# Expert operands asked for earlier in the order of a block, and one constant tile put at the head of its pool

## The chip, the cores and the metric

One core of a Trainium2 chip runs the kernel. The metric is the device time of one execution in microseconds. The engines are TensorE (PE in the profile, with its weight loads as PEld), VectorE (DVE), ScalarE (ACT), GpSimd (POOL) and SyncE (SP), which here only issues DMAs. Each engine works through its own queue in order and waits for the others by semaphores.

## What is computed

Three layers follow each other: linear attention with an exponential feature map, a soft mixture of experts with four slots for each of eight experts, and a dense mixture of eight experts whose weights P come from a gate that is normalised over rows and columns eight times. Only the last one matters here:

```python
def _moe2_ref(x, w_gate, w1, w2):        # x: 2304 x 512, 8 experts, hidden width 1024
    logits = x @ w_gate
    P = np.exp(logits - logits.max())
    for _ in range(8):
        P /= P.sum(1, keepdims=True) + 1e-09
        P /= P.sum(0, keepdims=True) + 1e-09
        P *= N / E
    out = np.zeros((N, D), dtype=np.float32)
    for e in range(E):
        h = np.maximum(x @ w1[e], 0.0)
        ye = h @ w2[e]
        out += P[:, e:e + 1] * ye
    return out
```

## The kernel before

**First layer.** The second layer's output has only 32 distinct rows behind it (its slots), so x is never formed: x @ w1[e] is the 2304 x 32 matrix of combine weights times a small product of slot outputs and w1[e]. The combine weights lie transposed in five tiles, ct0 to ct3 with 512 tokens each and ct4 with the last 256 (line 520 on). Each value is split into a high and a low part, stacked over the 128 rows. For an expert, `make_stack` computes the small product (matmuls ps, 32 of them), splits it, and `spread_stack` brings it into the form `st` that the first layer takes as its stationary operand (matmuls pr, two copies st<-pr on ACT). `first_layer(i, n)` is four matmuls of 256 tokens against ct; a block has two of these, together eight matmuls z<-ct,st.

**Blocks and products.** Tokens go in nine blocks of 256 for each expert, 72 blocks i in all, block after block and expert after expert (e, blk). The second layer, h @ w2[e], is one step of a scheme that needs seven products of half-size matrices instead of eight. Products 0 to 6 use the left operands a11, a12, s2, s1, s3, s4, a22 (made from the block's hidden values by `hidden`) and the right operands b11, b21, t2, t1, t3, b22, t4 (made from w2[e]). In the profile a right operand is w_b where it is a block of w2 itself (operands 0, 1, 5) and w_t where it is a sum (2, 3, 4, 6). Products 0, 2, 4 and 6 go into the sum x, 1 into z, 3 and 5 into y. Each product is 12 matmuls of 128 x 128 against 256 columns: four parts of the hidden width, each with high times high, high times low and low times high. After each product DVE adds its share, scaled by P, to the output tile xo (`take`). The sums lie in four PSUM buffers that are taken in turn.

**Hidden values.** `hidden(i + 1)` runs during block i. It is a generator of five steps, one after each of the products 2 to 6, and its first step comes after the first layer of block i + 1, which stands behind product 2 of block i. It makes r22, s1, s2, r11, s4, s3 as raw tiles (tag s, three buffers, so that s4 takes over the buffer of s1 and s3 that of s2), the high parts hh on ACT, and the low parts hl: those of a11, a12, a22 on DVE, those of s1, s2, s4, s3 on POOL (hl_s).

**Right operands.** The loop is written out by hand: from line 505 on, every instruction stays in program order on its engine, and all of them carry line 50 in the profile, that of the helper that records them. Two tables say behind which product of which block the next expert's operands are asked for:

```python
    W_SUMS = {(3, 1): 0, (3, 6): 1, (5, 6): 2, (7, 6): 3}
    W_PARTS = {(2, 6): 0, (4, 6): 2, (6, 6): 1, (8, 1): 3, (8, 6): 4, (9, 0): 5, (9, 1): 6}
```

A key is (block, product); blocks from 9 on mean blocks of the expert itself, so (9, 1) is behind product 1 of its own block 0. `w_sum(e, n)` is one subtraction or addition of 128 x 1024 on POOL: sum 0 makes t1 in the place of b11, sum 1 t2, sum 2 t3 in the place of b12, sum 3 t4 in the place of b21. `w_part(e, k)` makes operand k: a cast on ACT (its high part) and a subtraction on POOL (its low part). The operands lie in ten buffers, and operand k of expert e takes buffer (7e + k) mod 10. So operand 3 takes the buffer of the running expert's operand 0, 4 that of 1, 5 that of 2 and 6 that of 3; the last reader of each is that product in block 8.

**Order within a turn of the loop.** After product k and its take come, in this order: the next expert's stack (block 8, behind product 0) and its spreading (behind product 1), the next first layer (behind product 2), a step of `hidden`, a sum, a part, and two scalings of output rows on ACT in expert 0's block 8 and in expert 1.

**Weights.** SP loads the two units of w2 and the two of w1 of the next expert at the end of block 0 (1 MB each), into buffers that are freed when the last operand of the running expert has been made.

**The pool const.** It is the first pool on its side and lives for the whole kernel. Its tiles lie behind each other in the order in which their tags are first used: ident, ones (512 bytes per partition each), wg (128), si (2048), x0 to x5 (2048 each; later ct0 to ct3 and rep0, rep1 in the same places), rd_held (line 279; 16 bytes, which take 32), ct4 (1024). It begins at byte 16512 of a partition, and ct4 at 32032.

Of the kernel before, what the change touches and what calls it, by code (L numbers as in the profile page):

```python
# [8 lines left out]
F32R = mybir.dt.float32r  # L9
# [44 lines left out]
def tile_kernel(ctx: ExitStack, tc: tile.TileContext, a):  # L54
# [3 lines left out]
    const = ctx.enter_context(tc.tile_pool(name="const", bufs=1, side="left"))  # L58
# [8 lines left out]
    def load_const(name, shape, pool=None, q=SP):  # L67
        t = (pool or const).tile(shape, F32, name=name, bufs=1)
        q.dma_start(out=t, in_=a[name])
        return t  # L70
# [32 lines left out]
    def load_k(t):  # L103
        x = kp.tile([128, 512], F32, tag="kt", name=f"kt{t}")
        SP.dma_start(out=x, in_=a["kT"][t])
        kt_t[t] = x

    def load_v(i):
        x = kp.tile([128, 512], F32, tag="vt", name=f"vt{i}", bufs=3)
        SP.dma_start(out=x, in_=a["vb"][i])  # L110
        vt_t[i] = x
# [287 lines left out]
    load_k(1)  # L399
    load_v(0)  # L400
    load_k(2)
    ident = load_const("ident", [128, 128])
    ones = load_const("ones", [128, 128])
    sel_e = load_const("sel_e", [128, 4], kp)
# [113 lines left out]
    mp = mp_cm.__enter__()  # L518

    ct = [const.tile([128, 512], F32R, tag=f"x{i}", name=f"ct{i}", bufs=1) for i in range(4)]  # L520
    ct.append(const.tile([128, 256], F32R, name="ct4", bufs=1))
    rep = [const.tile([128, 4, 128], F32R, tag=f"x{4 + i}", name=f"rep{i}", bufs=1) for i in range(2)]
    for i in range(2):
        G.dma_start(out=rep[i], in_=a["rep"][:, i * 512:(i + 1) * 512].rearrange("p (g c) -> p g c", g=4))
# [99 lines left out]
    def w_sum(e, n):  # L624


        w = wsrc[e]
        if n == 0:
            G.tensor_tensor(out=w["t1"], in0=w["t3"], in1=w["b11"], op=ALU.subtract)
        elif n == 1:  # L630
            G.tensor_tensor(out=w["t2"], in0=w["t1"], in1=w["b22"], op=ALU.subtract)
        elif n == 2:
            G.tensor_tensor(out=w["t3"], in0=w["t3"], in1=w["b22"], op=ALU.subtract)
        else:
            G.tensor_tensor(out=w["t4"], in0=w["t4"], in1=w["t2"], op=ALU.add)

    def w_part(e, k):

        name = PRODUCTS[k][1]
        s = wsrc[e][name]  # L640
        n = (7 * e + k) % NW
        w = (cl1 if n < 4 else cl2).tile([128, 2, KH, 256], F32R, tag=f"wo{n}", name=f"w{e}_{name}", bufs=1)
        A.copy(out=w[:, 0], in_=s)
        G.tensor_tensor(out=w[:, 1], in0=s, in1=w[:, 0].bitcast(F32), op=ALU.subtract)
        wop[e, k] = w
        if k == 6:
            wsrc.pop(e)
            for n in range(2):
                unit_t.pop(("moe2_w2", e, n))
# [284 lines left out]
        pass  # L934
    load_munits(4)

    W_SUMS = {(3, 1): 0, (3, 6): 1, (5, 6): 2, (7, 6): 3}
    W_PARTS = {(2, 6): 0, (4, 6): 2, (6, 6): 1, (8, 1): 3, (8, 6): 4, (9, 0): 5, (9, 1): 6}
    SINK = {1: 3, 5: 2}
    making = iter(())  # L940
    for i, (e, blk) in enumerate(blocks):
# [3 lines left out]
        for k in range(7):  # L945
# [10 lines left out]
            next(making, None)  # L956
            if more and (blk, k) in W_SUMS:
                w_sum(e + 1, W_SUMS[blk, k])
            if more and (blk, k) in W_PARTS:
                w_part(e + 1, W_PARTS[blk, k])  # L960
            if e and (blk + 9, k) in W_PARTS:
                w_part(e, W_PARTS[blk + 9, k])
            if e == 0:
# [72 lines left out]
```

## Time and profile before

| | us |
|---|---|
| median of 3 runs | 1088.23 |
| lowest and highest | 1085.76, 1088.39 |
| the profiled execution, its own time | 1086.3 |
| its span, first to last instruction | 1084.1 |
| mean granted TensorE clock (share of full speed) | 0.995 |

| engine | busy, share of the span | instructions |
|---|---|---|
| PE | 1052.2 us, 97% | 9206 |
| DVE | 732.0 us, 68% | 1518 |
| POOL | 687.3 us, 63% | 442 |
| ACT | 569.8 us, 53% | 1009 |

The attention takes the first 230 us, the second layer's experts the stretch up to some 270 us, and the loop over 72 blocks the rest. Matmuls are pipelined: a record of 0.28 us follows the one before it after 0.11 us, so that the start of one to the start of the next is the measure of PE's pace, and a merged line of the timeline ("x8") gives the start of its first. In the timeline the brackets hold the engine's idle time before the line and what ended it. In the chain, a piece is a run of instructions of one kind, each following on the one before.

### The profile page before, as it was taken

How to read it: one execution, taken by the hardware profiler on the slowest of the kernel's cores; microseconds unless marked ns; L12 is line 12 of the kernel's file. 1: busy time of each engine (PE TensorE's matmuls, PEld its weight loads, DVE VectorE, ACT ScalarE, POOL GpSimd, SP SyncE). 2: the span in 40 equal slices, each digit the busy share in tenths (PEclk: the TensorE clock that was granted, in tenths of full speed). 3: DMA queues.
4: the chain of work that ended last, by engine and by line, in shares of the span. 5: the costliest groups of instructions: out<-in, count | busy, mean ns of one | idle time of the engine just before them, and what ended most of it. 6: DMA issues, size and time to landing. Idle time of an engine off the chain costs nothing.

```text
span 1084.1 us, 23152 instructions
## 1 busy us (share of the span) xinstructions
PE 1052.2 (97%) x9206; PEld 982.0 (91%) x9206; DVE 732.0 (68%) x1518; ACT 569.8 (53%) x1009; POOL 687.3 (63%) x442
## 2 busy tenths in 40 slices
PE   7999999999899999999999999999999999999998
PEld 5688788853899999999999999999999999999998
DVE  6878777850578767665766666576667666665765
ACT  5665544312556576654556454655555564545542
POOL 4776551107556777777777577767777775777443
PEclk9999999999899999999999999999999999999999
DMA  7772115379400130022003100300220031000111
GB/s 264 246 272 88 54 40 205 146 279 399 158 2 2 36 121 1 2 79 79 2 1 117 40 2 16 141 2 1 79 79 1 2 112 46 2 1 21 54 45 60
DMA packets 22571, 89.26 MB, mean 82 GB/s; under 512 B 2752, under 2 KB 5568, under 8 KB 14272
## 3 DMA queue, kind: packets, MB, share of 16 engines
q1 hardware_dynamic: 22176, 87.26, 22.2%
q8 instruction: 73, 1.20, 0.5%
q0 software_dynamic: 288, 0.52, 0.2%
q14 instruction: 34, 0.28, 0.1%
HBM read 83.05 MB, written 4.72 MB: 81 GB/s over the span
## 4 chain that ended last, share of the span: by engine, by line
PE 78%; POOL 11%; DVE 5%; issue 2%; DMA 2%; ACT 1%; SPq 0%; POOLq 0%; DVEq 0%; ACTq 0%
PE x L50 30%; PE y L50 14%; PE z L50 12%; PE num L271 6%; POOL hl_s L50 5%; POOL w_t L50 3%; PE kvacc L179 3%; POOL w_b L50 2%; PE ut L246 1%; PE ps L50 1%; DVE s L50 1%; PE kvp L218 1%; DMA moe_w<-in_moe_w 1%; PE pk L142 1%; PE ph L50 1%
## 5 line engine op out<-in xcount | busy, mean ns | idle before, releaser
L50 POOL TENSOR_TENSOR hl_s<-s,hh_s 128x512 fp32r<-128x512 f32 x288 | 367.5, 1298 | 230.1 <-ACT hh_s L50 214.0
L50 PE MATMUL x<-w_t,hh_s 128*128 128x256 f32 x1152 | 205.4, 278 | 3.9 <-DVE xo L50 2.7
L50 ACT ACTIVATE hh_s<-s 128x512 fp32r<-128x512 f32 x288 | 175.7, 629 | 53.0 <-DVE s L50 49.1
L50 PEld LDWEIGHTS x<-w_t,hh_s 128*128 128x128 f32 x1152 | 173.8, 188 | 5.3 <-issue 3.9
L50 DVE SCALAR_TENSOR_TENSOR xo<-x,P,xo 128x256 f32<-128x256 f32 x252 | 121.1, 481 | 75.3 <-PE x L50 75.3
L50 ACT ACTIVATE hh_a<-z 128x512 fp32r<-128x512 f32 x216 | 122.2, 600 | 90.1 <-DVE s L50 88.3
L50 ACT ACTIVATE r<-z 128x512 f32<-128x512 f32 x144 | 86.1, 598 | 156.6 <-PE z L50 156.2
L50 PE MATMUL x<-w_t,hl_s 128*128 128x256 f32 x576 | 159.7, 277 | 0.0
L50 DVE SCALAR_TENSOR_TENSOR s<-z,r 128x512 f32<-128x512 f32 x144 | 98.9, 687 | 86.7 <-ACT hh_a L50 82.2
L50 DVE SCALAR_TENSOR_TENSOR hl_a<-z,hh_a 128x512 fp32r<-128x512 f32 x216 | 147.4, 683 | 0.0
L50 DVE SCALAR_TENSOR_TENSOR s<-z,s 128x512 f32<-128x512 f32 x144 | 98.5, 684 | 19.4 <-POOL hl_s L50 17.9
L50 PE MATMUL x<-w_t,hh_a 128*128 128x256 f32 x576 | 104.2, 279 | 6.3 <-POOL w_t L50 4.9
L50 PEld LDWEIGHTS x<-w_t,hl_s 128*128 128x128 f32 x576 | 108.3, 188 | 0.0
L50 PE MATMUL y<-w_b,hh_s 128*128 128x256 f32 x576 | 103.8, 278 | 0.2 <-POOL w_b L50 0.2
L50 PE MATMUL x<-w_b,hh_a 128*128 128x256 f32 x576 | 103.1, 279 | 0.0
L50 PE MATMUL z<-w_b,hh_a 128*128 128x256 f32 x576 | 103.0, 279 | 0.0
L50 PE MATMUL y<-w_t,hh_s 128*128 128x256 f32 x576 | 102.9, 278 | 0.0
L50 PEld LDWEIGHTS x<-w_t,hh_a 128*128 128x128 f32 x576 | 87.5, 188 | 7.9 <-POOL w_t L50 6.2
L50 PEld LDWEIGHTS z<-w_b,hh_a 128*128 128x128 f32 x576 | 87.3, 189 | 2.9 <-issue 2.9
L50 PEld LDWEIGHTS y<-w_b,hh_s 128*128 128x128 f32 x576 | 87.5, 188 | 1.4 <-POOL w_b L50 1.3
L50 PEld LDWEIGHTS x<-w_b,hh_a 128*128 128x128 f32 x576 | 87.7, 190 | 0.0
L50 PEld LDWEIGHTS y<-w_t,hh_s 128*128 128x128 f32 x576 | 87.6, 188 | 0.0
(213 smaller groups left out, 2342.1 us busy)
## 6 DMA issues: line engine op xcount, KB each, us to landing
moe_w<-in_moe_w SPq DMA_DIRECT2D x64, 1024.0 KB, 6.9
vt<-in_vb SPq DMA_DIRECT2D x20, 256.0 KB, 3.7
kt<-in_kT SPq DMA_DIRECT2D x18, 256.0 KB, 3.1
qt<-in_qT SPq DMA_DIRECT2D x18, 256.0 KB, 2.8
out<-xo SPq DMA_DIRECT2D x18, 128.0 KB, 1.7
out<-xo SPq DMA_DIRECT2D x9, 256.0 KB, 2.0
rep<-in_rep POOLq DMA_DIRECT2D x2, 256.0 KB, 5.8
bd<-in_bd SPq DMA_DIRECT2D x1, 384.0 KB, 4.3
```

What stands on the lines that cost most here:

```text
L50: return lambda *args, **kwargs: self.tc.keep_in_program_order(make(*args, **kwargs))
L142: PE.matmul(o, hi[:, s], wbdh, start=True, stop=False)
L179: PE.matmul(acc[64 * j:64 * j + 64, p * 256:(p + 1) * 256], v[:, (2 * p + j) * D:(2 * p + j + 1) * D], phik[:, 2 * p + j].rearrange("p c f ...
L218: PE.matmul(ps[:, c * 192:(c + 1) * 192], kvt[:, p * 256 + c * 128:p * 256 + (c + 1) * 128], bd[:, p], start=True, stop=True)
L246: PE.transpose(ps[:, j * 128:(j + 1) * 128], uq_t[t][hh][:, j * 128:(j + 1) * 128], ident)
L271: PE.matmul(ps[r0:r1, j * XW:(j + 1) * XW], phiq[:, c, j * 128 + r0:j * 128 + r1], kvs_t[b][:, c, 4 * hh + j, :], start=c == 0, stop=c == 1,)
```

## The change

Two entries of the order of sums and operands move, and the tile ct4 is allocated before the other constants instead of in their wake. Sum 3 is asked for behind product 1 of block 7 (before: product 6), operand 3 behind product 0 of block 8 (product 1), operand 4 behind product 1 (product 6), operand 5 behind product 6 of block 8 (product 0 of the new expert's block 0), and operand 6 behind product 0 of the new block 0 (product 1).

```diff
@@ -399,6 +399,7 @@
     load_k(1)
     load_v(0)
     load_k(2)
+    ct4 = const.tile([128, 256], F32R, name="ct4", bufs=1)
     ident = load_const("ident", [128, 128])
     ones = load_const("ones", [128, 128])
     sel_e = load_const("sel_e", [128, 4], kp)
@@ -518,7 +519,7 @@
     mp = mp_cm.__enter__()
 
     ct = [const.tile([128, 512], F32R, tag=f"x{i}", name=f"ct{i}", bufs=1) for i in range(4)]
-    ct.append(const.tile([128, 256], F32R, name="ct4", bufs=1))
+    ct.append(ct4)
     rep = [const.tile([128, 4, 128], F32R, tag=f"x{4 + i}", name=f"rep{i}", bufs=1) for i in range(2)]
     for i in range(2):
         G.dma_start(out=rep[i], in_=a["rep"][:, i * 512:(i + 1) * 512].rearrange("p (g c) -> p g c", g=4))
@@ -934,8 +935,8 @@
         pass
     load_munits(4)
 
-    W_SUMS = {(3, 1): 0, (3, 6): 1, (5, 6): 2, (7, 6): 3}
-    W_PARTS = {(2, 6): 0, (4, 6): 2, (6, 6): 1, (8, 1): 3, (8, 6): 4, (9, 0): 5, (9, 1): 6}
+    W_SUMS = {(3, 1): 0, (3, 6): 1, (5, 6): 2, (7, 1): 3}
+    W_PARTS = {(2, 6): 0, (4, 6): 2, (6, 6): 1, (8, 0): 3, (8, 1): 4, (8, 6): 5, (9, 0): 6}
     SINK = {1: 3, 5: 2}
     making = iter(())
     for i, (e, blk) in enumerate(blocks):
```

## Rows read from the trace of the kernel before

**Rows 1.** The page, busy time of each engine.
```profile
PE 1052.2 (97%) x9206; PEld 982.0 (91%) x9206; DVE 732.0 (68%) x1518; ACT 569.8 (53%) x1009; POOL 687.3 (63%) x442
```

**Rows 2.** Who waited for whom, PE: us in total, times, longest.
```profile
PE x L50 <- POOL w_t L50: 4.9, 7, 0.7
```

**Rows 3.** Timeline of PE, first layers of eight blocks: start, us.
```profile
380.77 1.11 PE L50 MATMUL z<-ct,st 128*128 128x256 f32 x8
...
466.44 1.12 PE L50 MATMUL z<-ct,st 128*128 128x256 f32 x8
...
480.18 1.11 PE L50 MATMUL z<-ct,st 128*128 128x256 f32 x8
...
490.66 1.11 PE L50 MATMUL z<-ct,st 128*128 128x256 f32 x8
...
503.15 1.11 PE L50 MATMUL z<-ct,st 128*128 128x256 f32 x8
...
524.11 1.11 PE L50 MATMUL z<-ct,st 128*128 128x256 f32 x8
...
534.59 1.11 PE L50 MATMUL z<-ct,st 128*128 128x256 f32 x8
...
978.23 1.11 PE L50 MATMUL z<-ct,st 128*128 128x256 f32 x8
```

**Rows 4.** Timeline of POOL, expert 1's block 7 to expert 2's block 0.
```profile
465.55 2.40 POOL L50 TENSOR_TENSOR w_b<-moe_w,w_b 128x1024 fp32r<-128x1024 f32 x1
469.81 2.54 POOL L50 TENSOR_TENSOR hl_s<-s,hh_s 128x512 fp32r<-128x512 f32 x2 [1.85 <-ACT hh_s L50]
...
476.05 2.40 POOL L50 TENSOR_TENSOR moe_w<-moe_w,t 128x1024 f32<-128x1024 f32 x1
480.65 2.41 POOL L50 TENSOR_TENSOR w_t<-moe_w,w_t 128x1024 fp32r<-128x1024 f32 x1 [2.20 <-ACT w_t L50]
483.55 2.56 POOL L50 TENSOR_TENSOR hl_s<-s,hh_s 128x512 fp32r<-128x512 f32 x2 [0.49 <-ACT hh_s L50]
...
489.78 2.41 POOL L50 TENSOR_TENSOR w_t<-moe_w,w_t 128x1024 fp32r<-128x1024 f32 x1
...
494.50 2.41 POOL L50 TENSOR_TENSOR w_t<-moe_w,w_t 128x1024 fp32r<-128x1024 f32 x1
496.84 2.57 POOL L50 TENSOR_TENSOR hl_s<-s,hh_s 128x512 fp32r<-128x512 f32 x2
```

**Rows 5.** Timeline of PE, three places between 474 and 498 us.
```profile
474.55 1.93 PE L50 MATMUL ps<-moe_w,sot 128*32 128x256 f32 x32
...
494.34 0.67 PE L50 MATMUL y<-w_b,hh_s 128*128 128x256 f32 x2
...
496.96 0.39 PE L50 MATMUL x<-w_t,hh_a 128*128 128x256 f32 x1 [0.70 <-POOL w_t L50]
```

**Rows 6.** Timeline of DVE: low part of a12 (block 8), s4 (block 1).
```profile
471.00 0.68 DVE L50 SCALAR_TENSOR_TENSOR hl_a<-z,hh_a 128x512 fp32r<-128x512 f32 x1
...
498.19 0.69 DVE L50 SCALAR_TENSOR_TENSOR s<-z,s 128x512 f32<-128x512 f32 x1 [2.33 <-POOL hl_s L50]
```

**Rows 7.** Chain that ended last, 440 to 480 us: start, us, what.
```profile
457.06 1.38 PE y L50 x12
...
461.16 2.72 PE x L50 x24
...
471.80 2.83 PE x L50 x24
```

**Rows 8.** Busy time of each engine by stretch, then granted clock and DMA.
```profile
400.00:500.00 100.00, 98.84 (x873) 97.22 (x872) 67.29 (x129) 62.35 (x106) 71.88 (x47) 1.00 0.13 45
```

**Rows 9.** Timeline of POOL, expert 2's block 3: sum 0, hl_s.
```profile
525.70 2.41 POOL L50 TENSOR_TENSOR moe_w<-moe_w 128x1024 f32<-128x1024 f32 x1
528.06 2.57 POOL L50 TENSOR_TENSOR hl_s<-s,hh_s 128x512 fp32r<-128x512 f32 x2
```

**Rows 10.** Timeline of ACT: copy of the stack, cast of operand 3.
```profile
478.55 1.08 ACT L50 CAST st<-pr 128x512 fp32r<-128x512 f32 x2 [4.55 <-PE pr L50]
479.51 1.06 ACT L50 CAST w_t<-moe_w 128x1024 fp32r<-128x1024 f32 x1
```

## The prediction

> **What bounds the kernel now.** I read the page first. PE is busy for 1052.2 of 1084.1 us [rows 1]. So the kernel is bound by TensorE, and a change can only win where PE stands still or where its matmuls come at a longer spacing. Both kinds of loss exist, and both lie in the part that the diff touches, the expert loop, which fills the span from about 280 us on.
>
> The second view, who waited for whom on PE, has at its head only 4.9 us, for a weight operand that POOL makes, 7 times: once per change of expert [rows 2]. That sum is too small a measure, because a late operand also delays what stands behind it. So I measured the loop by its own beat, the start of each block's first layer (eight matmuls z<-ct,st). An undisturbed block takes 490.66 - 480.18 = 10.48 us [rows 3]. The block after it, the one that straddles block 0 and block 1 of a new expert, takes 503.15 - 490.66 = 12.49. The block that makes the next expert's stack takes 480.18 - 466.44 = 13.74. For all experts at once: from the first layer of expert 1 to that of expert 7, six experts, 978.23 - 380.77 = 597.46 us. Taking off 6 x (7 x 10.48 + 13.74) = 522.60 leaves 74.86, or 12.48 for the long one. **Each of seven expert changes loses 2.00 us, together 14.0.**
>
> **Why it is lost.** POOL's queue around the change from expert 1 to 2 [rows 4]: the low half of operand 3 ends at 480.65 + 2.41 = 483.06, then come the low parts of block 0's sums, from 483.55, and from 489.78 to 496.91 the low halves of operands 4, 5 and 6 without a pause (three of some 2.4 us). Only then come the low parts of block 1's s1 and s2, at 496.84 (records overlap by some 0.05 us). Two things follow. PE stands 0.70 us in product 6 of block 0, until operand 6 is there [rows 5]; and DVE waits 2.33 us for POOL before it can make s4 [rows 6], since s4 takes over the buffer of s1. DVE's takes stand behind that in its queue, and PE needs their PSUM buffers at block 1's second product. That is the rest of the 2.00.
>
> The second loss is in the spacing. 24 matmuls take 2.72 us in an ordinary block and 2.83 in the stretch after block 8's first layer, and likewise at the end of the last expert [rows 7]; a row of 2.82 or 2.83 at this place stands in all eight experts. That is 113.3 against 117.9 ns each, and the granted clock is 1.00 over both [rows 8]. Block 8's first layer is the only one that reads ct4; everything else at that place is as in other blocks.
>
> **The change part by part.** Nothing is added or removed: two Python entries of the order move, and one tile gets another place.
>
> *Sum 3 (t4), from product 6 to product 1 of block 7.* One POOL instruction of 2.40 us, the duration of its kind. It now follows operand 1's low half (465.55 to 467.95; operand 1 is w_b there) [rows 4] and so ends near 470.3, while block 8's first hl_s used to start at 469.81 in an idle engine: hl_s is 0.5 us late. What hides it: DVE makes s4 after the low part of a12, which ends at 471.00 + 0.68 = 471.68 [rows 6], and the first hl_s, 1.3 us long, now ends at 471.6. The trace also holds the same situation: sum 0, asked at (3,1) behind operand 0 of (2,6), keeps hl_s back until 528.06, 3.95 us after the first layer at 524.11, and the block still took 534.59 - 524.11 = 10.48 [rows 3, 9]. Here it would be 470.3 - 466.44 = 3.9. Cost: 0. Without that cover it is the 0.5 us, seven times 3.5.
>
> *Operand 3, from (8,1) to (8,0).* Cast on ACT (1.06 us) and subtraction on POOL (2.40). Its buffer, slot (7e+3) mod 10, is the one that operand 0 of the running expert holds until product (8,0) is over, near 474.55, when the stack's matmuls start [rows 5]. So the cast gets a wait on PE, at the head of ACT's queue. Behind it there is only the copy of the stack, which today starts at 478.55 after 4.55 us in which ACT waits for PE [rows 10]. The cast would run from 474.6 to 475.7, POOL's half after block 8's last hl_s, from 476.1 to 478.5, the time in which today it makes sum 3 (476.05) [rows 4]. Cost: 0; if it blocked ACT it would have to be 2.9 us later to touch the stack.
>
> *Operand 4, from (8,6) to (8,1).* It takes over exactly the place of operand 3: cast at 479.51 behind the stack's copy [rows 10], POOL at 480.65 [rows 4]. Its slot is free at the end of product (8,1), before pr. Cost: 0.
>
> *Operands 5 and 6, to (8,6) and block 0's product 0.* They take POOL's places of today's 4 and 5: 489.78 to about 492.1, and from there to 494.50. PE wants operand 5 at 494.34 [rows 5] and operand 6 one product (1.36) later, 495.7: 2.2 and 1.2 us to spare. Block 1's hl_s then starts at 494.50 instead of 496.84, which is 3.84 us behind the first layer at 490.66: less than the 3.95 that block 4 bore without loss. So the full 2.00 per change goes. Nearest rows from both sides: 0 left (block 4's row), or 0.5 us left each, if hl_s, still 0.5 behind its ordinary time (469.81 - 466.44 = 3.37 after the first layer), delays s3 and the takes behind it. I take 0 because that row is the same queue in the same state. **Term: -14.0 us, bounds -10.5 and -14.0.** The DMA queue on SP: the next weight loads go out when operand 6 releases its source, now 2.4 us sooner, and nothing waits for them.
>
> *ct4 at the head.* const is laid out in order of first use: ident, ones, wg, si, x0 to x5, then rd_held, whose 16 bytes take 32, then ct4. The pool starts at byte 16512, a multiple of 128; ct0 to ct3 lie at multiples of 128, ct4 at 32032, a multiple of 32 only. At the head it gets 16512, the rest moves up by 1024, and the pool's end stays. I take the odd place as the cause of the longer spacing, because place is the one difference between block 8's first layer and the others. One matmul costs (2.83 - 2.72) / 24 = 4.6 ns more [rows 7]. In experts 0 to 6 it lasts over five products of 12, until the stack's matmuls: 60 x 4.6 = 0.27 us, less the 0.02 that the first y loses in any block (1.38 [rows 7], where 12 x 113.3 is 1.36): 0.25. In the last expert, which makes no stack, it lasts over eleven products: 132 x 4.6 = 0.61, less 0.02: 0.59. That is 7 x 0.25 + 0.59 = 2.3. **Term: -2.3 us, bounds 0 and -2.3.** On the Trainium skill's page "SBUF — State Buffer", section "Specifications (TRN2)", the unit in which SBUF is read is a line of 16 bytes, and only each further line costs. Both 32032 and 16512 begin such a line, so by that rule the place would be all the same, and the sum -14.0 alone, as in rival (a); no row here shows a read that tells places finer than 32 bytes apart.
>
> **Sum.** -16.3. The profiled execution took 1086.3 us (span 1084.1 and 2.2 around it), the median is 1088.2, the fastest 1085.8. 1086.3 - 16.3 = 1070.0; from the median 1071.9. I forecast 1071.0.
>
> **Rivals.** (a) ct4's spacing stays, the cause being another than its place: only the 14.0 comes, 1072.3 from the profiled time, about 1073 from between the two. For it: why a first layer should set the spacing of later products no row explains. Against it: eight of eight. Chance 0.12. (b) Operand 3's cast does not get away before the stack's copy, say because its slot is released later than at product (8,0): the change then does not do what it says. Operand 4's half would run from 483.06 ahead of block 0's hl_s (483.55 today [rows 4]), which would be 1.9 us late; today 2.3 us of lateness cost 2.00 together with the waits for operands, so about 1.0 stays each time, 7 in all: 1078. Against it: the slot's last reader in the code is (8,0). Chance 0.06. (c) hl_s stays a little late at both places and takes 0.2 to 0.6 us per change: 1073 to 1075; chance 0.12. (d) Slower: moving const by 1024 bytes brings ct0 to ct3 into places like ct4's old one. Then 64 more blocks run at the longer spacing, each with 84 matmuls, 84 x 4.6 ns less what the first y loses anyway, 0.37 us: +24 - 14 = +10, 1096. It decides where the place counts on a grid over 1024 bytes. Against it: the two halves of each ct lie 1024 bytes apart, are read by even and odd blocks, and both give 2.72 [rows 7]. Chance 0.02.
>
> **How the numbers follow.** The likeliest case, both terms in full, has 0.66; 0.02 is for mishaps that end near no change. A difference under 0.3% (3.3 us) can hardly be told from none with this kernel. Cases faster by more: 0.66 + 0.12 + 0.06 + 0.12 = 0.96; within: 0.02; slower: 0.02. The range runs from 1067.5 (the fastest run less 16.3, and 2 us for what the beat may hide) to 1076.0 (case c with the median as its base); (b) and (d) are left out.
>
> **What would show it.** Right: the first-layer beat of every expert's block 0 to 1 at 10.48; no PE wait for w_t; operand 3's POOL half near the end of block 8's hl_s, before the stack's copy; DVE's wait for POOL before s4 gone at expert changes; every x24 row at 2.72. Wrong for ct4: 2.83 still behind block 8's first layer. Wrong for the parts: a beat over 10.6 there, or a new wait in block 8, in front of ps or pr. An expert's period should fall from 99.6 to 97.3.

## The result and the profile after

The changed kernel takes 1073.76 us (median of 4 runs, 1070.06 to 1076.59) against 1087.05 for the one before (4 runs, 1085.76 to 1088.39). The ratio is 0.9876, with a 95% interval of 0.9841 to 0.9911. The profiled execution took 1073.0 us with a span of 1070.8; before it was 1086.3 and 1084.1, so the two profiles lie 13.3 us apart.

The page of the changed kernel, busy time of each engine (as [rows 1]):

```profile
PE 1044.6 (98%) x9206; PEld 978.2 (91%) x9206; DVE 733.4 (68%) x1518; ACT 571.9 (53%) x1009; POOL 687.6 (64%) x442
```

The number of instructions is the same to the last one. Next, the changed kernel's first layers around the change from expert 1 to 2 in PE's timeline, as [rows 3]:

```profile
480.31 1.11 PE L50 MATMUL z<-ct,st 128*128 128x256 f32 x8
...
490.79 1.11 PE L50 MATMUL z<-ct,st 128*128 128x256 f32 x8
...
501.27 1.11 PE L50 MATMUL z<-ct,st 128*128 128x256 f32 x8
```

Both steps are 10.48 us; the second was 12.49 before. It is 10.48 at all seven expert changes. POOL's timeline of the same place, as [rows 4]:

```profile
465.90 2.40 POOL L50 TENSOR_TENSOR w_b<-moe_w,w_b 128x1024 fp32r<-128x1024 f32 x1
468.37 2.41 POOL L50 TENSOR_TENSOR moe_w<-moe_w,t 128x1024 f32<-128x1024 f32 x1
470.74 2.55 POOL L50 TENSOR_TENSOR hl_s<-s,hh_s 128x512 fp32r<-128x512 f32 x2
...
476.54 2.39 POOL L50 TENSOR_TENSOR w_t<-moe_w,w_t 128x1024 fp32r<-128x1024 f32 x1
480.79 2.40 POOL L50 TENSOR_TENSOR w_t<-moe_w,w_t 128x1024 fp32r<-128x1024 f32 x1 [1.85 <-ACT w_t L50]
...
489.90 2.40 POOL L50 TENSOR_TENSOR w_b<-moe_w,w_b 128x1024 fp32r<-128x1024 f32 x1
492.26 2.41 POOL L50 TENSOR_TENSOR w_t<-moe_w,w_t 128x1024 fp32r<-128x1024 f32 x1
494.62 2.55 POOL L50 TENSOR_TENSOR hl_s<-s,hh_s 128x512 fp32r<-128x512 f32 x2
```

The reader sees sum 3 (at 468.37) in the gap ahead of hl_s, operand 3 at 476.54 in sum 3's old place, and only two operands where three stood: hl_s of block 1 starts at 494.62, 3.83 us behind the first layer. In DVE's timeline s4 of block 1 follows without a wait (as the second of [rows 6]):

```profile
495.31 0.68 DVE L50 SCALAR_TENSOR_TENSOR hl_a<-z,hh_a 128x512 fp32r<-128x512 f32 x1
495.96 0.69 DVE L50 SCALAR_TENSOR_TENSOR s<-z,s 128x512 f32<-128x512 f32 x1
```

The chain of the changed kernel, 440 to 480 us, as [rows 7]. The rows at 467.89 and 471.99 lie behind block 8's first layer:

```profile
461.49 2.72 PE x L50 x24
...
467.89 1.38 PE y L50 x12
...
471.99 2.72 PE x L50 x24
```

The longer spacing is gone. Among who waited for whom on PE (us in total, times, longest) no operand from POOL is left, as against [rows 2]; the largest sum in the expert loop is now that for takes:

```profile
PE x L50 <- DVE xo L50: 2.8, 2, 1.4
```

One of the two is new: 1.4 us between 366 and 376 us, in expert 0's block 8; the other, in its block 4, stood in the trace of before as well. The steps from first layer to first layer of expert 0 (blocks 0, 4 and 8, the last up to expert 1's first) show where:

| step, us | before | after |
|---|---|---|
| expert 0, block 0 | 9.27 | 10.25 |
| expert 0, block 4 | 12.45 | 12.41 |
| expert 0, block 8 | 14.44 | 15.91 |
| the block that makes the stack, experts 1 to 6 | 13.74 | 13.54 |
| expert changes, mean of 7 (before: 12.31 to 12.60) | 12.46 | 10.48 |
| block 8's first layer to the last matmul, expert 7 | 16.39 | 15.82 |

The balance of the two profiles: seven expert changes -13.9; ct4 -0.20 in each of seven experts and -0.57 at the end, -2.0; a new stall in expert 0's block 8 +1.66 (15.91 against 14.25, which other runs below give); block 0 of expert 0 +0.98, the start of the loop -0.26, expert 6's block 5 +0.19. Together -13.3.

The longer block 0 of expert 0 is no work of the change: the granted clock is not 1.00 throughout there, part of the stretch runs at 1.2 instead of 2.4 GHz. The stretch from 276 to 292 us, before and after in this order (busy time of each engine, then granted clock, DMA share, GB/s):

```profile
276.00:292.00 16.00, 13.41 (x97) 12.94 (x98) 9.26 (x20) 8.27 (x17) 8.00 (x6) 0.89 0.66 259
```

```profile
276.00:292.00 16.00, 13.96 (x91) 13.28 (x92) 8.21 (x18) 8.18 (x16) 9.13 (x6) 0.79 0.65 257
```

Over this step alone the mean granted clock was 0.82 before and 0.69 after. In all the traces here the step took 9.27 to 9.30 us where it was 0.82 and 9.51 to 10.37 where it was 0.57 to 0.70, and the loop began between 276.8 and 282.8 us, both in no relation to the edits. That can be much of the scatter of some 5 us that single executions show (only one of each kernel left a trace), and it is why the small terms below are read from steps of the loop and not from whole times.

### The profile page after: what moved, and what is told of

Same layout as the page of the kernel before. It is cut to its first block, busy times and chain, and to the rows that moved or that the text cites. A ratio compares the mean times of both kernels' runs of the same rounds, so it can differ in the third digit from the quotient of the medians.

```text
span 1070.8 us, 23152 instructions
## 1 busy us (share of the span) xinstructions
PE 1044.6 (98%) x9206; PEld 978.2 (91%) x9206; DVE 733.4 (68%) x1518; ACT 571.9 (53%) x1009; POOL 687.6 (64%) x442
## 4 chain that ended last, share of the span: by engine, by line
PE 90%; DVE 4%; POOL 2%; DMA 2%; issue 1%; ACT 0%; SPq 0%; DVEq 0%; POOLq 0%; ACTq 0%
PE x L50 36%; PE y L50 18%; PE z L50 15%; PE num L271 6%; PE kvacc L179 3%; PE ut L246 1%; PE ps L50 1%; DMA moe_w<-in_moe_w 1%; PE kvp L218 1%; PE pk L142 1%; PE ph L50 1%; PE pk L144 1%; PE pk L143 1%; PE pq L142 1%; PE pq L144 1%
## 5 line engine op out<-in xcount | busy, mean ns | idle before, releaser
L50 PE MATMUL x<-w_t,hh_a 128*128 128x256 f32 x576 | 101.8, 277 | 2.8 <-DVE xo L50 2.8
L50 PE MATMUL y<-w_b,hh_s 128*128 128x256 f32 x576 | 101.5, 276 | 0.0
```

The costliest lines, as they stand in the source:

```text
L50: return lambda *args, **kwargs: self.tc.keep_in_program_order(make(*args, **kwargs))
```

## The experiments

My theories: expert changes were late because POOL had three halves of operands in front of hl_s; ct4's place set the spacing; the new stall of expert 0 comes from sum 3. Times below are medians; those of the first four stand against 1085.65 us for the kernel before, run beside them.

**The order alone.** ct4 stays where it was; only the two tables change, in five places (sum 3 and operands 3 to 6).

> The new order of sums and operands alone; ct4 stays at byte 32032. Theory, POOL's queue: the beat from block 0's to block 1's first layer falls to 10.48 us at all seven expert changes (12.3 to 12.6 before), 13.9 us together; the 24-matmul row behind block 8's first layer stays at 2.83; expert 0's block 8 keeps a new stall of some 1.6 us; so about 1086.3 - 13.9 + 1.6 = 1074.0 in all, and the last expert's tail still takes 16.4 us from block 8's first layer to the last matmul. Rival, the two parts of the change need each other (the beat is only mended with ct4 moved): a beat above 11.

1075.06 us, ratio 0.9903 (0.9879 to 0.9926). All seven expert changes at 10.48; the step with the stack 13.74, and 2.82 in the chain behind block 8's first layer; tail 16.39; expert 0's block 8 15.93. The row of the chain behind block 8's first layer in expert 1:

```profile
471.19 2.82 PE x L50 x24
```

The parts work without ct4.

**ct4 alone.** The old tables, ct4 at the head.

> ct4 at the head, the old order of sums and operands. Theory, the place of ct4 sets the spacing: 2.72 in every 24-matmul row behind block 8's first layer, the beat with the stack 13.54 (13.74 before), the last expert's tail 15.8 (16.4 before), together 0.2 x 7 + 0.57 = 2.0 us, within what the runs scatter; expert changes stay at 12.3 to 12.6. Rival, the spacing changed for another reason (the order of operands): 2.83 and 13.74 stay.

1084.34 us, ratio 0.9994 (0.9975 to 1.0013): by whole times nothing to see. The steps show it all the same: 13.54 with the stack in experts 1 to 6, tail 15.82, expert changes still 12.37 to 12.64. 7 x 0.20 + 0.57 = 2.0 us. The row of the same place:

```profile
470.11 2.72 PE x L50 x24
```

**Sum 3 back.**

```diff
-    W_SUMS = {(3, 1): 0, (3, 6): 1, (5, 6): 2, (7, 1): 3}
+    W_SUMS = {(3, 1): 0, (3, 6): 1, (5, 6): 2, (7, 6): 3}
```

> The changed kernel with sum 3 back behind product 6 of block 7. Theory, the new stall of expert 0's block 7 comes from two POOL operations back to back that hold up DVE's gate normalisation: the beat of expert 0's block 8 falls from 15.91 to about 14.25, DVE's TENSOR_SCALAR on rs there from 1.97 to 0.18 us, all expert changes stay at 10.48, and the kernel gains 1.6 us on the changed one. Rival, sum 3 has to be early to leave POOL room in block 8: with it late, the low halves of operands 3 and 4 come later and expert changes lose 0.5 us or more each (beat 11 or more).

1070.20 us, ratio 0.9866 (0.9826 to 0.9906). Expert 0's block 8 takes 14.25, all expert changes 10.48. The early sum bought nothing and cost 1.66 us.

**Operands 3 and 4 alone.**

```diff
-    W_SUMS = {(3, 1): 0, (3, 6): 1, (5, 6): 2, (7, 1): 3}
-    W_PARTS = {(2, 6): 0, (4, 6): 2, (6, 6): 1, (8, 0): 3, (8, 1): 4, (8, 6): 5, (9, 0): 6}
+    W_SUMS = {(3, 1): 0, (3, 6): 1, (5, 6): 2, (7, 6): 3}
+    W_PARTS = {(2, 6): 0, (4, 6): 2, (6, 6): 1, (8, 0): 3, (8, 1): 4, (9, 0): 5, (9, 1): 6}
```

> The changed kernel with only operands 3 and 4 asked for earlier; sum 3 and operands 5 and 6 as before. Theory, POOL's queue: what helps is that block 8's idle POOL time takes one more operand; 5 and 6 follow from that, since their casts were done long before POOL came to them, so the beat at expert changes is 10.48 as with the full change, and the time equals that of the kernel with sum 3 back, within 1 us. Rival, each operand must be asked for earlier for itself: operand 6, asked behind product 1 of block 0, is late and PE waits for it, beat 11 to 12.

1072.56 us, ratio 0.9879 (0.9856 to 0.9902). Every expert change at 10.48, expert 0's block 8 at 14.25. Against the kernel with sum 3 back the profiled span is 1.8 us longer (1070.2 and 1068.4), all of it ahead of the loop's second block: the loop began 0.81 us later, and its first block took 10.27 instead of 9.27. From there to the last matmul it is 775.50 and 775.54 us. So asking for 5 and 6 earlier brings nothing of its own; the whole gain of the order is that two operands instead of one go into block 8.

**Gate steps moved.** First try at the new stall, and a miss.

```diff
-                for _ in range(SINK.get(k, 0) - (blk == 0 and k == 1)):
+                for _ in range({5: 5}.get(k, 0) if blk == 7 else SINK.get(k, 0) - (blk == 0 and k == 1)):
```

> The changed kernel, sum 3 early as it is, but in expert 0's block 7 the three steps of the gate normalisation behind product 1 are taken behind product 5 together with the two there. Theory, DVE's TENSOR_SCALAR is shut out for as long as POOL's sum runs: with no such operation of DVE between 366 and 371 us the beat of expert 0's block 8 goes from 15.91 to about 14.3, although hl_s of block 8 starts as late as before. Rival, it is hl_s being 0.5 us late that makes s4 and the takes late: the beat stays near 15.9.

Expert 0's block 8 took 18.45 us, the kernel 1074.67 in one run. The steps moved behind product 5 begin with a matmul of the gate, and PE waited 2.17 us before it, as its timeline shows:

```profile
373.70 0.36 PE L50 MATMUL pcs<-cs,ones 128*128 128x8 f32 x2 [2.17 <-DVE s L50]
```

Behind that wait the granted clock was 0.50 from 374.9 to 378.3 us, which made the block longer still. The edit put a stall of its own where the old one had been, so it decides nothing.

**Without the addition of 1e-9.**

```diff
             V.tensor_reduce(out=rs, in_=P, axis=AX.X, op=ALU.add)
-            V.tensor_scalar_add(rs, rs, 1e-9)
             V.reciprocal(out=rs, in_=rs)
```

> The changed kernel, sum 3 early as it is, without the addition of 1e-9 to the row sums of the gate (one TENSOR_SCALAR of DVE in each of eight rounds is left out; it is the one that took 1.97 instead of 0.18 us where POOL had two operations back to back). Theory, DVE is shut out by POOL for that instruction: the beats of expert 0 fall from 12.41 to 10.8 (block 4) and from 15.91 to 14.3 (block 8), with hl_s starting as late as before. Rival, the late hl_s alone: 12.4 and 15.9 stay.

1065.51 us in a single run. Expert 0's block 4 takes 10.76 and its block 8 14.25, with sum 3 still early and still ahead of hl_s, as POOL's timeline in this kernel shows:

```profile
363.03 2.40 POOL L50 TENSOR_TENSOR moe_w<-moe_w,t 128x1024 f32<-128x1024 f32 x1
365.45 2.56 POOL L50 TENSOR_TENSOR hl_s<-s,hh_s 128x512 fp32r<-128x512 f32 x2
```

So the instruction on DVE costs it all. My expectation that hl_s would start as late as before was a miss: it starts 4.00 us behind the first layer (at 361.45), as in the kernel with sum 3 back (4.00), while in the changed kernel it is 5.56 (372.58 after 367.02), since there POOL waits 1.62 us for ACT's hh_s, which waits for DVE's s. So this run does not show what a late hl_s alone costs; experts 1 to 6 do, where sum 3 makes hl_s 0.6 us later (3.97 in expert 1, 3.37 with sum 3 back) and the block takes 13.54 either way. The timelines of the changed kernel's DVE and then POOL at that place:

```profile
368.69 0.30 DVE L50 TENSOR_REDUCE rs<-P 128x18 f32<-128x144 f32 x1
369.02 1.97 DVE L50 TENSOR_SCALAR rs<-rs 128x18 f32<-128x18 f32 x1
371.03 0.27 DVE L50 RECIPROCAL rs<-rs 128x18 f32<-128x18 f32 x1
```

```profile
366.10 2.39 POOL L50 TENSOR_TENSOR w_b<-moe_w,w_b 128x1024 fp32r<-128x1024 f32 x1
368.57 2.39 POOL L50 TENSOR_TENSOR moe_w<-moe_w,t 128x1024 f32<-128x1024 f32 x1
372.58 2.53 POOL L50 TENSOR_TENSOR hl_s<-s,hh_s 128x512 fp32r<-128x512 f32 x2 [1.62 <-ACT hh_s L50]
```

In DVE's timeline of the kernel with sum 3 back the same instruction takes 0.18 us:

```profile
368.50 0.18 DVE L50 TENSOR_SCALAR rs<-rs 128x18 f32<-128x18 f32 x1
```

In the changed kernel it ends when POOL's sum ends (370.99 and 370.96). DVE's queue behind it, the products' takes among it, moves back by 1.8 us, and PE waits 1.4 us for a take. The trace of before had the same thing in expert 0's block 4, where sum 0 follows operand 0; DVE's timeline, then POOL's:

```profile
320.95 2.25 DVE L50 TENSOR_TENSOR P<-P,cs 128x144 f32<-128x144 f32 x1
323.24 0.30 DVE L50 TENSOR_REDUCE rs<-P 128x18 f32<-128x144 f32 x1
323.58 1.97 DVE L50 TENSOR_SCALAR rs<-rs 128x18 f32<-128x18 f32 x1
```

```profile
320.64 2.39 POOL L50 TENSOR_TENSOR w_b<-moe_w,w_b 128x1024 fp32r<-128x1024 f32 x1
323.12 2.40 POOL L50 TENSOR_TENSOR moe_w<-moe_w 128x1024 f32<-128x1024 f32 x1
```

One POOL operation holds the multiplication of P (2.25 us where others take 0.30) without loss: it is held in the kernel with sum 3 back too (2.27 us), whose block 8 takes 14.25. A second operation right behind the first holds the next such instruction. The Trainium skill's page "SBUF — State Buffer", section "Who interferes with whom", has this: VectorE and GpSimd share a port pair, and a VectorE instruction with two SBUF inputs, or a tensor_scalar in its two-port mode, waits for the whole of a GpSimd instruction that reads SBUF and was issued first, while a tensor_reduce does not. The rows agree in all three: 2.25, 1.97 and 0.30 us beside a busy POOL; which mode the tensor_scalar ran in, no row shows.

**No two of POOL's operations back to back.** All sums and operands of before block 8 get a place of their own.

```diff
-    W_SUMS = {(3, 1): 0, (3, 6): 1, (5, 6): 2, (7, 1): 3}
-    W_PARTS = {(2, 6): 0, (4, 6): 2, (6, 6): 1, (8, 0): 3, (8, 1): 4, (8, 6): 5, (9, 0): 6}
+    W_SUMS = {(2, 6): 0, (3, 6): 1, (5, 6): 2, (7, 6): 3}
+    W_PARTS = {(2, 1): 0, (4, 6): 2, (6, 6): 1, (8, 0): 3, (8, 1): 4, (8, 6): 5, (9, 0): 6}
```

> The changed kernel with POOL's sums and operands spread so that no two of them stand back to back before block 8: operand 0 behind product 1 of block 2, sum 0 behind product 6 of block 2, sum 3 behind product 6 of block 7. Theory: both long beats of expert 0 are gone, 12.41 to 10.8 and 15.91 to 14.25, the expert changes stay at 10.48: 3.3 us less than the changed kernel, 1.6 less than the one with sum 3 back. Rival, the stall of block 4 is not POOL's pair of operations: 12.4 stays. Or the early operand 0 is held up by its weights' landing: a stall in block 2.

1070.73 us (1068.04 to 1071.16), ratio 0.9846 (0.9813 to 0.9878) against 1087.04 for the kernel before, run beside it; the changed kernel's ratio was 0.9876. Expert 0's block 4 takes 10.76 and its block 8 14.25, no block 2 is longer. By steps of the loop that is 3.3 us less than the changed kernel; by whole times the two intervals overlap.

**The place of ct4.** Three trials missed in the same way. Two of them add unused bytes around ct4, in the changed kernel (`ct4_off32`: 32 before, 32 behind) and in the one before (`ct4_mid`: rd_held of 64 bytes, 32 behind ct4); the third (`w_at_64`) is the kernel before with rd_held of 64 bytes and nothing more.

> The changed kernel with 32 unused bytes before ct4 at the head of const and 32 behind it, so that ct4 begins at 16544, a multiple of 32 only, and everything else keeps its distance to multiples of 64. Theory, the place within 64 bytes: the longer spacing is back, 2.83 for 24 matmuls behind block 8's first layer, beat with the stack 13.74, last tail 16.4. Rival, being at the head is what helps: 2.72, 13.54, 15.8.

> The kernel before, with rd_held given 64 bytes instead of 32 (and 32 unused bytes behind ct4), so that ct4 comes to byte 32064, a multiple of 64, without leaving its place in the order; what lies behind const keeps its distance to multiples of 64. Theory, what counts is where ct4 begins within 64 bytes: spacing as with ct4 at the head, beat with the stack 13.54, last tail 15.8. Rival, the head of the pool or a multiple of 128 is needed: 13.74 and 16.4.

> The kernel before with rd_held given 64 bytes and nothing behind ct4: ct4 comes to a multiple of 64, and so do the right operands of the products and the units of weights (69952 for the first, 69920 before). Theory, a first layer at a multiple of 64 brings the short spacing whatever follows: 10.48 in ordinary blocks, 13.54 with the stack. Rival, the short spacing comes from a first layer whose place within 64 bytes differs from that of the products' operands: all alike now, it is lost everywhere, and an ordinary block takes 10.85, 24 us in all.

They took 1109.40, 1112.71 and 1109.12 us in one run each (the kernel before: 1086.18), since all ordinary blocks grew: 11.01, 11.01 and 10.88 us instead of 10.48. I had kept the distance of everything behind const to multiples of 64 in the first two, but not to 128; the right operands had moved. Neither theory had that. The rival of the third named 10.85 for its kernel, on another ground: that right operands which lie like the first layer's bring the longer spacing. Its own kernel does not refute it; the other two, where they do not lie alike within 64 bytes for ct0 to ct3, are slower still. The clean trial moves ct4 by 32 and all the rest by 128:

```diff
+    const.tile([128, 8], F32, name="pad0", bufs=1)
     ct4 = const.tile([128, 256], F32R, name="ct4", bufs=1)
+    const.tile([128, 24], F32, name="pad1", bufs=1)
```

> The changed kernel with 32 unused bytes before ct4 and 96 behind it: ct4 begins at 16544, 32 past a multiple of 128 as in the kernel before, and everything else moves by a whole 128 bytes. Theory, ct4's place within 128 bytes sets the spacing that follows: 2.83 for 24 matmuls behind block 8's first layer, beat with the stack 13.74, last tail 16.4; ordinary blocks stay at 10.48. Rival, being at the head is what helps: 2.72, 13.54, 15.8.

The chain of this kernel in expert 2: an ordinary block, the same place behind block 8's first layer, and the stack:

```profile
566.90 2.72 PE x L50 x24
...
577.52 2.83 PE x L50 x24
580.35 1.86 PE ps L50 x32
```

With ct4 at the head but 32 past a multiple of 128, the longer spacing is back: step with the stack 13.80 or 13.81 in experts 1 to 6, tail 16.37. So the place of ct4, not the head of the pool, makes the difference; the kernel took 1083.65 us in one run. What it is about the place stays open: at 32 past a multiple of 128 ct4 lies as the products' right operands do, in all three kernels where the longer spacing stood behind it, and its own place was not tried apart from that. One thing came that neither theory had: the ordinary blocks of experts 0 and 1 run at the longer spacing as well (11.07 and 10.85 us), and two of expert 6 behind its block 5; those of experts 2 to 5 and 7 take 10.48. In the kernel before and with the order alone a first layer on ct0 to ct3 always brought the short spacing back; here, with these tiles 128 bytes further on, it did not. Why is open.

**Right operands at a multiple of 128.** The evenly spread kernel with 96 unused bytes at the end of const.

> As the one above, with 96 unused bytes at the end of const, so that the products' right operands begin at a multiple of 128 (70016), where they were 32 past one (69920) at 113.3 ns, 64 past (69952) at 118.3 and 96 past (69984) at 120.0; the left operands stay at 96 past. Theory, the distance between the two operands that PE reads, within 128 bytes, sets the spacing: 64 apart is the best (113.3), 0 the worst (120.0), 96 between; 32 apart would be as 96, about 118, an ordinary block 10.9. Rival, it is the place of the right operand alone and a multiple of 128 is the best: 113.3 or less, 10.48 or less.

1087.71 us, ratio 1.0014 (0.9995 to 1.0034): an ordinary block takes 10.77 us instead of 10.48, and all that the order had won is spent. The 24-matmul rows of the chain in four kernels, with the place of the products' right operands modulo 128: 32 (`even`), 0 (`even_w96`), 64 (`w_at_64`) and 96 (`ct4_mid`).

```profile
406.99 2.72 PE x L50 x24
```

```profile
405.35 2.80 PE x L50 x24
```

```profile
413.69 2.84 PE x L50 x24
```

```profile
410.67 2.88 PE x L50 x24
```

That is 113.3, 116.7, 118.3 and 120.0 ns for a matmul, the same matmuls in the same order on PE. The rival, a multiple of 128 as the best place, falls; the theory's own 10.9 was not met either. The left operands (hh and hl) lie at 96 in all four, so 64 bytes between the two is the fast one and 0 the slow one; whether the distance counts or the place of the right one alone was not tried, since the left ones were never moved. Nor is the longer spacing of 117.8 kept apart: at 0 the right operands lie like ct0 to ct4 within 128 bytes, at 64 within 64, so these two figures may hold some of it. The 120.0 came with ct0 to ct3 at 0 (`ct4_mid`) and at 64 (`ct4_off32`) alike.

## Why the prediction was right, point by point

The forecast was 1071.0 us with a range of 1067.5 to 1076.0; measured 1073.76. The likeliest case came with its two terms and one addition that I had priced at nothing. Of the 3.0 us by which the two profiles fall short of the -16.3, 1.66 is that addition, 0.4 are the two terms, and 0.9 the start of the loop with its first block and expert 6's block 5, which no edit explains.

- **The expert changes, -14.0.** -13.9 measured. The reading by block 4's row, that 3.95 us between first layer and hl_s costs no time, held: 3.83 here, and all seven steps at 10.48. Operand 3 ran in sum 3's old place, operand 4 in operand 3's, as listed. What the working did not see is that operands 5 and 6 need not have been asked for sooner; the kernel with 3 and 4 alone has the same steps.
- **ct4, -2.3.** -2.0 measured in the profiles: 0.20 instead of 0.25 for each expert and 0.57 instead of 0.59 at the end. The 0.05 is in the product behind the stack: its 12 matmuls took 1.56 us in the chain before and 1.61 after, so part of what is won ahead of the stack is given back behind it. The cause given, the place, is borne out by the clean trial; that it is oddness, and not a place like that of the products' operands, is not shown. The Trainium skill's page "SBUF — State Buffer", section "Specifications (TRN2)", with lines of 16 bytes as the unit, would have had both places alike; the clean trial differs by 32 bytes, two such lines, and the measurement decides.
- **The step that failed: sum 3, "Cost: 0".** Right in experts 1 to 6, wrong in expert 0, where it cost 1.66 us. The row taken as proof, sum 0 in expert 2's block 3, has no gate normalisation beside it. The same pair of POOL operations in expert 0's block 4 stood in the same trace with a step of 12.45. The cover that I named (DVE busy anyway until 471.6) held for hl_s in experts 1 to 6, which is 0.6 us late there at no cost; what I missed is that POOL's instruction itself stops DVE's, 1.97 us where 0.18 would do.
- **The rivals.** (b), operand 3 held up, and (c), a rest of hl_s's lateness, did not come: operand 3's cast ran from 474.74, ahead of the stack's copy. (a) fell with the steps of 13.54. (d) did not come with 1024 bytes. What it did not name came with smaller moves: the products' right operands 32, 64 or 96 bytes further on cost 0.3 to 0.5 us in each block.

## What to carry to other kernels

Where an engine off the critical path holds up the others once per round, find the idle stretch of its queue and put one piece of work there; here the other pieces then came right by themselves. A row that proves a move free must have the same neighbours: look at every copy of the pattern in the trace, the one with the most going on beside it first. And an edit that changes a pool's size should keep the places of matmul operands, or the whole loop may change its pace.

## What was not expected of the hardware

- The spacing of matmuls of 128 x 128 by 256 columns went from 113.3 to 120.0 ns when the right operands moved by 64 bytes, at a granted clock of 1.00: 26.5 us on the kernel before (1086.18 and 1112.71 in single runs), and some 36 on the changed one (1109.40 in a single run against 1073.76).
- Two spacings, 113.3 and 117.8, occur with the same places. Which one runs depends on what ran before: in the changed kernel, in expert 6's block 5, it changed behind one step of 0.19 us from matmul to matmul (others 0.11), with no first layer between, and came back with the next first layer (that block took 10.76 us).
- A DVE instruction of 0.18 us on 18 values in each partition lasts 1.97 us when POOL's begins ahead of it, and that was worth 1.66 us of the kernel's time.
